# Attention of the later tiles: float32 products on quarters of the TensorE array instead of split float32r products

## The chip, the cores and the metric

The kernel runs on one core of one Trainium2 chip. The metric is device time in microseconds, from the start to the end of one execution. The kernel before takes 1346.17 us (median of 3 runs, 1345.73 to 1346.28).

## The reference, cut to what matters

Eight batches of 576 tokens with 8 heads of 64 features: attention within chunks of 64 tokens, then two feed-forward blocks on 4608 tokens of 512 features.

```python
q_c = q.reshape(B, H, nc, 64, 64)                 # the same for k, v
scores = scale * np.matmul(q_c, k_c.transpose(0, 1, 2, 4, 3))
scores = scores - np.max(scores, axis=-1, keepdims=True)
attn = np.exp(scores)
attn = attn / (np.sum(attn, axis=-1, keepdims=True) + 1e-09)
x = np.matmul(attn, v_c)                          # heads side by side: 4608 x 512
xn = (x - mu) / np.sqrt(var + 1e-06) * g_ln
x2 = x + np.maximum(xn @ w_ch1, 0.0) @ w_ch2      # 512 -> 2048 -> 512
h = np.maximum(x2 @ w_in, 0.0)                    # 512 -> 1024
out = h * sigmoid(conv3(h)) @ w_out               # taps over tokens; 1024 -> 512
```

All data is float32.

## The kernel before, in words

**Tiles and slabs.** Tokens go through in 36 tiles of 128 (two chunks of 64 each) and in nine slabs of four tiles. Phase A does attention and the first feed-forward block, phase B the second one. This case lies in phase A.

**The dense work.** A float32 operand is split into hi + lo, twelve leading bits each, so that TensorE can use single-pass float32r; one product is three matmuls (`mm3`, lines 100 to 103). For one slab, 16 groups f of 128 hidden features go by: `U(f)` (line 591, 12 matmuls of 512 columns into the PSUM tile `ups`), `H(f)` (line 605, ScalarE: relu, hi), `K(f)` (line 610, VectorE: lo), and `D(f)` (line 614, 12 matmuls into the four `acc` tiles). In the program `D(f-1)` comes after `U(f)`. The PSUM tile of `ups` has two buffers; attention has one buffer of two banks, tag `at` (`at_bank2`), which scores, transposes, values and two of the four feature transposes `xtp` share in turn.

**Attention of the next slab lies between the dense matmuls.** The order is written out by hand. Slab 0 follows the list START: it computes the attention of tiles 0 to 7 by class `Whole` (lines 278 to 413), in plain float32. `Whole.S` (line 317) multiplies 128 rows of block-diagonal q by 64 columns of k for each of 8 heads. `Whole.V` (line 372) multiplies operands of 64 rows, alternately in the upper and the lower half of the array's rows. `Whole.P` (line 353) transposes in float32. A plain float32 matmul shows in the trace as two records, each with its own weight load.

In slabs 1 to 7 `slot(t)` is called twice per f, after `K(f)` (t = 2f) and after `D(f-1)` (t = 2f + 1), so 12 dense matmuls lie between two slots. It runs class `Split` (lines 415 to 529) for the next slab's four tiles, in eight jobs of one tile and one parity of heads, three slots each:

- `load` fetches q, k and v of the job, each twice (to both halves of the partitions): 12 DMAs of 128 KB per tile, on SP's queue.
- `prep_qk`, `prep_v`: hi on ScalarE (lines 440, 441, 97), lo on VectorE (lines 442, 445, 98).
- `S` (line 472): four matmuls with 128 rows (q's hi above q's lo) and 256 columns; `fold` (lines 462, 464) adds the parts; maxima.
- `exp` (line 487): four ACTIVATEs with sums, then the division (lines 491 to 493). `parts` splits the weights (lines 97, 98).
- `P` (line 507): four float32r transposes, copied out at line 512.
- `V` (line 523): four matmuls of 256 columns, `fold` into x; for the second parity the statistics of layer normalization.

On VectorE, `late` holds four stores of the slab before (line 630, a transpose of 128 x 512, then a DMA); one is issued after each of K(0) to K(3), ahead of the slot.

Slab 8 has no attention beside it, and phase B starts behind it.

Of the kernel before, what the change touches and what calls it, by code (L numbers as in the profile page):

```python
# [17 lines left out]
# The first slab, step by step, in an order in which each engine finds its next step ready. Of a  # L18
# tile: L load, S scores, M maxima, E exponentials, N weights, P C transposed, V values, X B x and
# its statistics, x normalized, T transposed, p q hi and lo. Of a piece of the weights: W load,  # L20
# a t m to float32, h l hi and lo. Of 128 hidden features: U up, H K hi and lo, D down.
# [18 lines left out]
def attn_moe_moe2(  # L40
# [16 lines left out]
    """Tokens go through in tiles of 128, two chunks of 64 each, and in slabs of four tiles.  # L57

    q0, k0, the first tiles: tile, chunk c, d, parity e of the head, pair j (head 2j + e), row of
    the chunk; q, k, the others: tile, parity, d, pair, chunk, row; v: tile, parity, row, pair,  # L60
    chunk, d.
    A float32 is split exactly into hi + lo, twelve leading bits each, for the tensor engine's
    single-pass float32r: a product is lo*hi + hi*lo + hi*hi.
    """
# [21 lines left out]
    ident_r = const.tile([128, 128], F32R, name="ident_r")  # L86
# [18 lines left out]
    # -------------------------------------------------------------- weights  # L105
# [3 lines left out]
    class Piece:  # L109
        """w as float32, times scale, split into hi + lo, which take the place of w as it came."""  # L110
# [47 lines left out]
    def top_bits(y, raw):  # L158
        """Of a float64's top word: the float32 but for its last three bits, shifted right by 3."""
        # Of the exponents' difference, 1023 - 127, 112 * 8.  # L160
        nc.scalar.activation(
            out=y.bitcast(F32), in_=raw[..., 1].bitcast(F32), func=AF.Copy, scale=2.0 ** -112
        )

    def low_bits(raw):
        """Of a float64's low word: the float32's last three bits, rounded, with at most 7."""
        nc.vector.tensor_scalar(
            out=raw[..., 0], in0=raw[..., 0].bitcast(U32), scalar1=2.0 ** -29, scalar2=7.0,
            op0=ALU.mult, op1=ALU.min,
        )  # L170

    def to_f32(y, raw):
        """The shift drops the sign; the top word has it."""
        nc.vector.scalar_tensor_tensor(
            out=y, in0=y, scalar=3, in1=raw[..., 0], op0=ALU.logical_shift_left, op1=ALU.bitwise_or
        )
        nc.vector.scalar_tensor_tensor(
            out=y, in0=raw[..., 1], scalar=-0x80000000, in1=y, op0=ALU.bitwise_and, op1=ALU.bitwise_or
        )
# [27 lines left out]
    def cv_step():  # L207
        """A step of each of three pieces."""
# [22 lines left out]
    def add(w, parts, at, pool, tag, scale=None):  # L231
        """The [128, 512] block w for parts[at]: hi, lo."""
# [25 lines left out]
    # ------------------------------------------------------------ attention  # L258
# [19 lines left out]
    class Whole:  # L278
        """Attention of a whole tile in float32: few steps for the vector engine."""

        def __init__(self):
            self.pool = tc.alloc_tile_pool(name="at1", bufs=1, side="right", reuse_waits="tile")
            own = self.pool.tile([128, H, 128], F32, name="qbd")
            # The first tiles' q, block diagonal, where their features will be.
# [130 lines left out]
    class Split:  # L415
        """Attention by jobs of one tile and one parity of heads, for the fewest passes.

        The rows of a product's operands are the twelve-bit parts of q (of the weights) over d
        (over the keys); the columns hold k's (v's) parts beside each other.
        """  # L420

        def __init__(self):
            self.p = tc.alloc_tile_pool(name="at2", bufs=1, side="right", reuse_waits="tile")
            self.raw, self.qk, self.vv, self.st, self.x = {}, {}, {}, {}, {}

        def load(self, j):
            T, e = divmod(j, 2)
            for nm, src in (("q", q), ("k", k), ("v", v)):
                t = self.p.tile([128, 512], F32, tag="rw", bufs=6, name="rw" + nm)
                a = src[T if nm == "v" else T - N0, e].rearrange("p j c s -> p (j c s)")  # L430
                for x in range(2):
                    nc.sync.dma_start(out=t[half(x)], in_=a)
                self.raw[nm, j] = t

        def prep_qk(self, j):
            qr, kr = self.raw.pop(("q", j)), self.raw.pop(("k", j))
            qs = self.p.tile([128, HP, 128], F32R, tag="qs", name="qs")
            ks = self.p.tile([128, 2, HP, 128], F32R, tag="ks", name="ks")
            qf, kf = (t.rearrange("p j n -> p (j n)") for t in (qs, ks[:, 0]))
            nc.scalar.copy(qf, qr)  # L440
            nc.scalar.copy(kf, kr)
            nc.vector.tensor_tensor(
                out=qf[half(1)], in0=qr[half(1)], in1=qf[half(1)].bitcast(F32), op=ALU.subtract
            )
            nc.vector.tensor_tensor(
                out=ks[:, 1].rearrange("p j n -> p (j n)"), in0=kr, in1=kf.bitcast(F32), op=ALU.subtract
            )
            self.qk[j] = (qs, ks)

        def prep_v(self, j):  # L450
            vr = self.raw.pop(("v", j))
            vs = self.p.tile([128, 2, HP, 128], F32R, tag="vs", name="vs")
            f = [vs[:, i].rearrange("p j n -> p (j n)") for i in range(2)]
            split(f[0], f[1], vr)
            self.vv[j] = vs

        def fold(self, out, ps):
            """out[row, head] = the sum over the parts of the row's own chunk."""
            pv = ps.rearrange("p b (j i c n) -> p (b j) i c n", j=2, i=2, c=2)
            t = self.p.tile([128, HP, 64], F32, tag="c1", bufs=2, name="c1")  # L460
            for c in range(2):
                nc.scalar.copy(t[half(c)], pv[half(c), :, 1, c, :])
            for c in range(2):
                nc.vector.tensor_tensor(
                    out=out[half(c)], in0=pv[half(c), :, 0, c, :], in1=t[half(c)], op=ALU.add
                )

        def S(self, j):
            qs, ks = self.qk.pop(j)
            ps = at_bank2("sp")  # L470
            for h in range(HP):
                nc.tensor.matmul(  # L472
                    ps[:, h // 2, (h % 2) * 256:(h % 2) * 256 + 256], qs[:, h, :], ks[:, :, h, :],
                    start=True, stop=True,
                )
            s = self.p.tile([128, HP, 64], F32, tag="s", bufs=2, name="s")
            self.fold(s, ps)
            mx = self.p.tile([128, HP], F32, tag="mx", bufs=2, name="mx")
            sm = self.p.tile([128, HP], F32, tag="sm", bufs=2, name="sm")
            nc.vector.tensor_reduce(out=mx, in_=s, axis=AX.X, op=ALU.max)  # L480
            nc.vector.tensor_scalar_mul(out=mx, in0=mx, scalar1=-SCALE)  # L481
            self.st[j] = (s, mx, sm)

        def exp(self, j):
            s, mx, sm = self.st[j]
            for h in range(HP):
                nc.scalar.activation(  # L487
                    out=s[:, h, :], in_=s[:, h, :], func=AF.Exp, scale=SCALE, bias=mx[:, h:h + 1],
                    accum_out=sm[:, h:h + 1],
                )  # L490
# [3 lines left out]
                out=s, in0=s, in1=sm[:, :, None].to_broadcast([128, HP, 64]), op=ALU.mult  # L494
            )

        def parts(self, j):
            s = self.st.pop(j)[0]
            ph = self.p.tile([128, HP, 2, 64], F32R, tag="ph", bufs=2, name="ph")
            split(ph[:, :, 0, :], ph[:, :, 1, :], s)  # L500
            self.st[j] = ph

        def P(self, j):
            ph = self.st.pop(j)
            tp = at_bank2("tp")[:, 0, :]
            for h in range(HP):
                nc.tensor.transpose(  # L507
                    tp[:, h * 128:(h + 1) * 128].bitcast(F32R),
                    ph[:, h].rearrange("p i k -> p (i k)"), ident_r,
                )  # L510
            pt = self.p.tile([128, HP, 128], F32R, tag="pt", name="pt")
            nc.scalar.copy(pt.rearrange("p h t -> p (h t)"), tp)
            self.st[j] = pt

        def V(self, j):
            T, e = divmod(j, 2)
            pt, vs = self.st.pop(j), self.vv.pop(j)
            if e == 0:
                self.x[T] = x_tile()
            x = self.x[T]  # L520
            ps = at_bank2("pv")
            for h in range(HP):
                nc.tensor.matmul(  # L523
# [4 lines left out]
            if e:  # L528
                ln_stats(T, self.x.pop(T))
# [427 lines left out]
```

## Time and profile before

| | |
|---|---|
| median of 3 runs | 1346.17 us (1345.73 to 1346.28) |
| the profiled execution, first to last instruction | 1345.0 us, 18441 instructions |
| TensorE (matmul records) busy | 1325.9 us, 99% |
| VectorE, ScalarE, GpSimd busy | 871.7, 702.8, 81.1 us |
| mean granted TensorE clock | 0.985 of full |
| DMA queue of the data, share of 16 engines | 24.8% |

The profiled execution is one execution of its own; the page gives its time from the first to the last instruction, 1345.0 us, which is 1.2 us under the median of the runs. Matmuls are pipelined and the ends of their records are modelled, so records overlap, and a busy share of 99% doesn't say that the array computes all the time. What an operation costs TensorE is read from the starts of records: from its own first start to the start of what follows.

### The profile page before, as it was taken

The numbers are of one execution on the slowest core, as the hardware profiler recorded it, in microseconds if no ns is written. First come the engines' busy times: TensorE is split into PE (matmuls) and PEld (weight loads), VectorE is DVE, ScalarE is ACT, GpSimd is POOL, SyncE is SP. The second block draws the span as 40 slices with busy tenths as digits, with TensorE's granted clock in tenths as the row PEclk, the third lists the DMA queues.
The fourth block names the chain that finished last, engine by engine and source line by source line (L and its number), as shares of the span: only waits on it lengthen the run. The fifth ranks groups of instructions, "written<-read, shape, count | busy, mean of one in ns | idle before, by whom it ended". The sixth has DMA issues, their size and how long they took to land.

```text
span 1345.0 us, 18441 instructions
## 1 busy us (share of the span) xinstructions
PE 1325.9 (99%) x6312; PEld 1100.1 (82%) x6312; DVE 871.7 (65%) x1824; ACT 702.8 (52%) x1767; POOL 81.1 (6%) x176
## 2 busy tenths in 40 slices
PE   7899999999999999999999999999999999999998
PEld 6788788888888888888888888888788888888887
DVE  6898577566666666676676676555787556655550
ACT  5675366365365365365365365233576555555541
POOL 1000000000000000000000000000022111111100
PEclk6799999999999999999999999999999999999999
DMA  9812042132132132132132133141311111101001
GB/s 290 334 53 59 16 126 79 43 99 79 44 98 79 46 96 79 47 95 79 48 94 79 47 95 80 40 164 63 94 39 41 48 55 63 49 30 56 24 24 47
DMA packets 77661, 105.04 MB, mean 78 GB/s; under 512 B 20224, under 2 KB 38656, under 8 KB 77568
## 3 DMA queue, kind: packets, MB, share of 16 engines
q1 hardware_dynamic: 77568, 103.87, 24.8%
q8 instruction: 50, 0.82, 0.3%
q14 instruction: 43, 0.35, 0.1%
HBM read 84.96 MB, written 18.87 MB: 77 GB/s over the span
## 4 chain that ended last, share of the span: by engine, by line
PE 93%; DVE 4%; ACT 1%; DMA 1%; issue 1%; SPq 1%; DVEq 0%; ACTq 0%
PE ups L101 14%; PE ups L103 14%; PE ups L102 14%; PE acc L101 10%; PE acc L103 10%; PE acc L102 10%; PE ops L102 5%; PE ops L103 5%; PE ops L101 5%; PE sp L472 2%; PE pv L523 2%; PE xtp L563 1%; PE tp L507 1%; PE sp L317 1%; DMA w<-in_moe_w_ch_dram 0%
## 5 line engine op out<-in xcount | busy, mean ns | idle before, releaser
L101 PE MATMUL ups<-xh,w 128*128 128x512 f32 x656 | 260.6, 397 | 1.4 <-ACT xh L406 1.4
L103 PE MATMUL ups<-xh,w 128*128 128x512 f32 x656 | 258.2, 394 | 0.0
L102 PE MATMUL ups<-xl,w 128*128 128x512 f32 x656 | 257.1, 392 | 0.3 <-DVE xl L410 0.3
L101 PE MATMUL acc<-w,hl 128*128 128x512 f32 x576 | 229.5, 399 | 0.0
L103 PE MATMUL acc<-w,hh 128*128 128x512 f32 x576 | 225.3, 391 | 0.0
L102 PE MATMUL acc<-w,hh 128*128 128x512 f32 x576 | 225.1, 391 | 0.0
L605 ACT ACTIVATE hh<-ups 128x512 fp32r<-128x512 f32 x144 | 86.3, 599 | 237.6 <-PE ups L103 230.8
L610 DVE SCALAR_TENSOR_TENSOR hl<-ups,hh 128x512 fp32r<-128x512 f32 x144 | 99.6, 691 | 153.1 <-ACT hh L605 151.5
L103 PEld LDWEIGHTS ups<-xh,w 128*128 128x128 f32 x656 | 123.6, 188 | 27.8
L101 PEld LDWEIGHTS ups<-xh,w 128*128 128x128 f32 x656 | 123.9, 189 | 25.4 <-ACT xh L406 2.0
L102 PEld LDWEIGHTS ups<-xl,w 128*128 128x128 f32 x656 | 123.8, 189 | 25.3 <-DVE xl L410 1.1
L103 PEld LDWEIGHTS acc<-w,hh 128*128 128x128 f32 x576 | 108.2, 188 | 23.9
L101 PEld LDWEIGHTS acc<-w,hl 128*128 128x128 f32 x576 | 108.2, 188 | 19.9
L102 PEld LDWEIGHTS acc<-w,hh 128*128 128x128 f32 x576 | 108.4, 188 | 19.3
L840 DVE SCALAR_TENSOR_TENSOR cv<-hb,cw_sb,cv 128x510 f32<-128x510 f32 (+31 forms) x256 | 117.2, 513 | 0.6
L102 PE MATMUL ops<-w,Gh 128*128 128x512 f32 x288 | 112.0, 389 | 0.0
L101 PE MATMUL ops<-w,Gl 128*128 128x512 f32 x288 | 112.0, 389 | 0.0
L103 PE MATMUL ops<-w,Gh 128*128 128x512 f32 x288 | 112.0, 389 | 0.0
L487 ACT ACTIVATE s<-s,mx 128x64 f32<-128x64 f32 x224 | 74.9, 337 | 54.9 <-DVE mx L481 54.9
L855 DVE SCALAR_TENSOR_TENSOR gt<-cv,hb 128x512 f32<-128x512 f32 (+2 forms) x72 | 49.6, 689 | 50.6 <-ACT cv L850 50.6
L870 ACT CAST Gh<-gt 128x512 fp32r<-128x512 f32 (+5 forms) x96 | 46.9, 512 | 61.5 <-DVE gt L855 61.5
L275 POOL TENSOR_TENSOR rs<-rs,mhalf 128x1 f32<-128x1 f32 x36 | 23.5, 652 | 819.4 <-DVE rs L274 819.4
(115 smaller groups left out, 2145.9 us busy)
## 6 DMA issues: line engine op xcount, KB each, us to landing
w<-in_moe_w_ch_dram SPq DMA_DIRECT2D x32, 512.0 KB, 8.8
rwq<-in_q_dram SPq DMA_DIRECT2D x112, 128.0 KB, 2.7
rwk<-in_k_dram SPq DMA_DIRECT2D x112, 128.0 KB, 2.7
rwv<-in_v_dram SPq DMA_DIRECT2D x112, 128.0 KB, 2.7
x2d<-x2T SPq DMA_DIRECT2D x36, 256.0 KB, 2.0
x2r<-x2d SPq DMA_DIRECT2D x36, 256.0 KB, 3.9
out_dram<-ob SPq DMA_DIRECT2D x36, 256.0 KB, 2.0
w<-in_moe_w_out_dram SPq DMA_DIRECT2D x8, 512.0 KB, 5.2
```

The source lines that it names most:

```text
L101: nc.tensor.matmul(ps, ll, rh, start=first, stop=False)
L102: nc.tensor.matmul(ps, lh, rl, start=False, stop=False)
L103: nc.tensor.matmul(ps, lh, rh, start=False, stop=last)
L275: nc.gpsimd.tensor_tensor(out=rs, in0=rs, in1=mhalf, op=ALU.pow)
L472: nc.tensor.matmul(ps[:, h // 2, (h % 2) * 256:(h % 2) * 256 + 256], qs[:, h, :], ks[:, :, h, :], start=True, stop=True,)
L487: nc.scalar.activation(out=s[:, h, :], in_=s[:, h, :], func=AF.Exp, scale=SCALE, bias=mx[:, h:h + 1], accum_out=sm[:, h:h + 1],)
L523: nc.tensor.matmul(ps[:, h // 2, (h % 2) * 256:(h % 2) * 256 + 256], pt[:, h, :], vs[:, :, h, :], start=True, stop=True,)
L605: nc.scalar.activation(out=hh, in_=ps, func=AF.Relu)
L610: nc.vector.scalar_tensor_tensor(out=hl, in0=ps, scalar=0.0, in1=hh.bitcast(F32), op0=ALU.max, op1=ALU.subtract)
L840: nc.vector.scalar_tensor_tensor(out=cv[:, a:e], in0=hb[:, a + tap:e + tap], scalar=cw_sb[:, tap, f:f + 1], in1=cv[:, a:e], op0=ALU.mult, ...
L855: nc.vector.scalar_tensor_tensor(out=self.gt[:, j0:j1], in0=self.cv[:, j0:j1], scalar=1.0, in1=self.hb[:, j0 + 1:j1 + 1], op0=ALU.add, op1 ...
L870: nc.scalar.copy(Gh[self.f][:, r], g)
```

## The change

Class `Quad` takes the place of `Split` for tiles 8 to 35. It works on whole tiles, in plain float32, without splitting anything.

- `load`: one DMA of 256 KB each for q, k and v of a tile: parity e of the heads lies in partitions 64e to 64e + 63, each once.
- `quarters` issues, for each of four pairs j, four matmuls of 64 rows, 64 stationary and 64 moving columns: parity e picks the half of the array's rows and the PSUM bank, chunk c the half of its columns and of the PSUM partitions. So a product of a tile is 16 matmuls, and nothing is computed that isn't used.
- `session(tv, ts)` issues the values of tile tv and then the scores of tile ts into one `at` tile (the scores in the first half of each bank, the values in the second), the maxima of ts on VectorE, and one ScalarE copy of the values.
- One slot later `exp(ts)` (eight ACTIVATEs that read PSUM), the statistics of tv, and the load of tile tv + 2; two slots later `norm(ts)` on VectorE; three slots later `P(ts)`: four float32 transposes and a ScalarE copy.
- The sessions lie in slots 2, 10, 18, 26 of a slab (2, 8, 14, 20, 26 in slab 1, of which the first has scores alone). The last one of slab 7 has values alone: 29 sessions.
- `ident_r`, the identity as float32r, and the ScalarE cast that wrote it go away. START, the dense work, slab 8 and phase B stay as they are; comments are blanked.

```diff
-    ident_r = const.tile([128, 128], F32R, name="ident_r")
...
-    class Split:
...
+    class Quad:
...
+        def load(self, T):
+            for nm, src, to in (("q", q[T - N0], self.q), ("k", k[T - N0], self.k), ("v", v[T], self.v)):
+                t = self.p.tile([128, HP, 2, 64], F32, tag="r" + nm, bufs=2, name="r" + nm)
+                nc.sync.dma_start(
+                    out=t.rearrange("p j c s -> p (j c s)"),
+                    in_=src.rearrange("e p j c s -> (e p) (j c s)"),
+                )
+                to[T] = t
+
+        def quarters(self, ps, lt, rt):
+            for j in range(HP):
+                for e, c in ((0, 0), (1, 1), (0, 1), (1, 0)):
+                    nc.tensor.matmul(
+                        ps[half(c), e, j, :], lt[half(e), j, c, :], rt[half(e), j, c, :],
+                        start=True, stop=True,
+                    )
+
+        def session(self, tv, ts):
+
+            both = at_bank2("sv").rearrange("p e (i j n) -> p e i j n", i=2, n=64)
+            if tv is not None:
+                self.quarters(both[:, :, 1], self.st.pop(tv), self.v.pop(tv))
+            if ts is not None:
+                self.quarters(both[:, :, 0], self.q.pop(ts), self.k.pop(ts))
+                mx = self.p.tile([128, 2, HP], F32, tag="mx", bufs=2, name="mx")
+                nc.vector.tensor_reduce(out=mx, in_=both[:, :, 0], axis=AX.X, op=ALU.max)
+                nc.vector.tensor_scalar_mul(out=mx, in0=mx, scalar1=-SCALE)
+                self.st[ts] = (both[:, :, 0], mx)
+            if tv is not None:
+                x = x_tile()
+                nc.scalar.copy(x.rearrange("p (j e) d -> p e j d", e=2), both[:, :, 1])
+                self.st[tv] = x
...
+        def norm(self, T):
+            pp, sm = self.st.pop(T)
             nc.vector.tensor_scalar_add(out=sm, in0=sm, scalar1=1e-9)
             nc.vector.reciprocal(out=sm, in_=sm)
             nc.vector.tensor_tensor(
-                out=s, in0=s, in1=sm[:, :, None].to_broadcast([128, HP, 64]), op=ALU.mult
+                out=pp, in0=pp, in1=sm[:, :, :, None].to_broadcast([128, HP, 2, 64]), op=ALU.mult
             )
...
+            if si == 1:
+                plan = {2: (None, n0), 8: (n0, n0 + 1), 14: (n0 + 1, n0 + 2), 20: (n0 + 2, n0 + 3),
+                        26: (n0 + 3, n0 + 4)}
+            else:
+                plan = {2: (n0, n0 + 1), 10: (n0 + 1, n0 + 2), 18: (n0 + 2, n0 + 3), 26: (n0 + 3, n0 + 4)}
...
+                for at, (tv, ts) in plan.items():
+                    if ts == NTILE:
+                        ts = None
+                    if t == at:
+                        at2.session(tv, ts)
+                    elif t == at + 1:
+                        if ts is not None:
+                            at2.exp(ts)
+                        if tv is not None:
+                            at2.stats(tv)
+                            if tv + 2 < NTILE:
+                                at2.load(tv + 2)
+                    elif t == at + 2 and ts is not None:
+                        at2.norm(ts)
+                    elif t == at + 3 and ts is not None:
+                        at2.P(ts)
```

## Rows read from the trace of the kernel before

**Rows 1.** The page: busy time of each engine; granted clock in 40 slices.

```profile
PE 1325.9 (99%) x6312; PEld 1100.1 (82%) x6312; DVE 871.7 (65%) x1824; ACT 702.8 (52%) x1767; POOL 81.1 (6%) x176
...
PEclk6799999999999999999999999999999999999999
```

**Rows 2.** Busy time of each engine in one slab, with granted clock and DMA share.

```profile
core 0: us, PE busy (x) PEld busy (x) DVE busy (x) ACT busy (x) POOL busy (x), PEclk, DMA share, GB/s
448.60:549.34 100.74, 100.66 (x499) 83.81 (x497) 66.87 (x148) 53.49 (x156) 2.33 (x4) 1.00 0.25 74
```

**Rows 3.** Waits of PE over the span, the longest row: us in total, times, longest us.

```profile
PE sp L317 <- DMA kr<-in_k_dram: 3.1, 2, 1.8
```

**Rows 4.** Timeline of PE, slab 2: start, us, what, count. Values, then scores.

```profile
301.14 0.63 PE L523 MATMUL pv<-vs,pt 128*128 128x256 f32 x4
301.61 0.39 PE L101 MATMUL ups<-xh,w 128*128 128x512 f32 x1
...
304.37 0.64 PE L472 MATMUL sp<-ks,qs 128*128 128x256 f32 x4
304.84 0.40 PE L101 MATMUL acc<-w,hl 128*128 128x512 f32 x1
```

**Rows 5.** Timeline of PE, slab 2: the transposes of one job.

```profile
307.59 0.45 PE L507 MATMUL tp<-ident_r,ph 128*128 128x128 f32 x4
...
308.18 0.39 PE L102 MATMUL ups<-xl,w 128*128 128x512 f32 x1
```

**Rows 6.** Timeline of PE, slab 0: plain float32 scores on all 128 rows.

```profile
115.44 1.90 PE L317 MATMUL sp<-kr,qbd 128*128 128x64 f32 x16
...
117.46 0.39 PE L102 MATMUL ups<-xl,w 128*128 128x512 f32 x1
```

**Rows 7.** Timeline of PE, slab 0: plain float32 values, on row halves.

```profile
122.48 0.39 PE L103 MATMUL acc<-w,hh 128*128 128x512 f32 x1
122.80 1.16 PE L372 MATMUL pv<-vt,pt 64*128 64x128 f32 x16
...
124.23 0.40 PE L102 MATMUL ups<-xl,w 128*128 128x512 f32 x1
```

**Rows 8.** Those values' weight loads begun by three times: window, busy (count).

```profile
122.79:122.81 0.02, 0.01 (x2) 1.00 0.00 0
122.79:123.01 0.22, 0.21 (x4) 1.00 0.00 0
...
122.79:123.23 0.44, 0.43 (x8) 1.00 0.00 0
```

**Rows 9.** Timeline of PE, slab 0: plain float32 transposes.

```profile
112.22 0.60 PE L353 MATMUL tp<-ident,pp 128*128 128x128 f32 x4
...
112.90 0.40 PE L102 MATMUL acc<-w,hh 128*128 128x512 f32 x1
```

**Rows 10.** Timeline, slab 2: last matmul of a U, its relu, its K.

```profile
297.78 0.39 PE L103 MATMUL ups<-xh,w 128*128 128x512 f32 x1
...
298.21 0.60 ACT L605 ACTIVATE hh<-ups 128x512 fp32r<-128x512 f32 x1 [2.01 <-PE ups L103]
...
298.84 0.69 DVE L610 SCALAR_TENSOR_TENSOR hl<-ups,hh 128x512 fp32r<-128x512 f32 x1 [1.09 <-ACT hh L605]
```

**Rows 11.** Timeline of DVE: maxima and division in slab 0; K and store in slab 2.

```profile
117.37 0.69 DVE L323 TENSOR_REDUCE mx<-sp 128x8 f32<-128x512 f32 x1 [0.39 <-PE sp L317]
...
120.87 0.17 DVE L342 TENSOR_SCALAR sm<-sm 128x8 f32<-128x8 f32 x1
...
121.31 0.69 DVE L344 TENSOR_TENSOR pp<-pp,sm 128x512 f32<-128x512 f32 x1
...
257.90 0.69 DVE L610 SCALAR_TENSOR_TENSOR hl<-ups,hh 128x512 fp32r<-128x512 f32 x1 [2.36 <-ACT hh L605]
258.51 0.70 DVE L630 STREAM_TRANSPOSE x2T<-x 128x512 f32<-128x512 f32 x1
259.13 0.82 DVE L464 TENSOR_TENSOR s<-sp,c 64x256 f32<-64x256 f32 x2
```

More of the change, by code (lines that the diff above doesn't have):

```diff
@@ L413, in q @@
             )
-    class Split:
+    class Quad:
         def __init__(self):
             self.p = tc.alloc_tile_pool(name="at2", bufs=1, side="right", reuse_waits="tile")
[L424 to L465, printed above, removed]
-                )
[L468 to L490, printed above, removed]
@@ new lines, in __init__ @@
+            self.q, self.k, self.v, self.st = {}, {}, {}, {}
+        def load(self, T):
[4 more added lines that the diff above has]
+                    in_=src.rearrange("e p j c s -> (e p) (j c s)"),
+                )
+                to[T] = t
@@ new lines, in exp @@
+        def exp(self, T):
+            sp, mx = self.st.pop(T)
+            sm = self.p.tile([128, HP, 2], F32, tag="sm", bufs=2, name="sm")
+            pp = self.p.tile([128, HP, 2, 64], F32, tag="pp", bufs=2, name="pp")
+            for j in range(HP):
+                for e in range(2):
+                    nc.scalar.activation(
+                        out=pp[:, j, e, :], in_=sp[:, e, j, :], func=AF.Exp, scale=SCALE,
+                        bias=mx[:, e, j:j + 1], accum_out=sm[:, j, e:e + 1],
+                    )
+            self.st[T] = (pp, sm)
@@ L491, in exp, with stats @@
+        def stats(self, T):
+            ln_stats(T, self.st.pop(T))
+        def norm(self, T):
+            pp, sm = self.st.pop(T)
             nc.vector.tensor_scalar_add(out=sm, in0=sm, scalar1=1e-9)
@@ L493, in exp, with P @@
             nc.vector.tensor_tensor(
-                out=s, in0=s, in1=sm[:, :, None].to_broadcast([128, HP, 64]), op=ALU.mult
+                out=pp, in0=pp, in1=sm[:, :, :, None].to_broadcast([128, HP, 2, 64]), op=ALU.mult
             )
[L497 to L504, printed above, removed]
+            self.st[T] = pp
+        def P(self, T):
+            pp = self.st.pop(T)
             tp = at_bank2("tp")[:, 0, :]
-            for h in range(HP):
+            for j in range(HP):
                 nc.tensor.transpose(
-                    tp[:, h * 128:(h + 1) * 128].bitcast(F32R),
-                    ph[:, h].rearrange("p i k -> p (i k)"), ident_r,
-                )
[L511 to L523, printed above, removed]
-                    ps[:, h // 2, (h % 2) * 256:(h % 2) * 256 + 256], pt[:, h, :], vs[:, :, h, :],
-                    start=True, stop=True,
-                )
-            self.fold(x.rearrange("p (j e) d -> p e j d", e=2)[:, e], ps)
-            if e:
-                ln_stats(T, self.x.pop(T))
+                    tp[:, j * 128:(j + 1) * 128], pp[:, j].rearrange("p e k -> p (e k)"), ident
+                )
+            pt = self.p.tile([128, HP, 2, 64], F32, tag="pt", bufs=2, name="pt")
+            nc.scalar.copy(pt.rearrange("p j c r -> p (j c r)"), tp)
+            self.st[T] = pt
     with tc.manual_schedule():
@@ L540, in attn_moe_moe2 @@
         nc.gpsimd.memset(mhalf, -0.5)
-        nc.scalar.copy(ident_r, ident)
         for f in range(NF1):
@@ L690, in attn_moe_moe2 @@
                 cvp.release()
-                at2 = Split()
-                at2.load(16)
-                at2.prep_qk(16)
-                at2.load(17)
+                at2 = Quad()
+                at2.load(N0)
+                at2.load(N0 + 1)
             if not nxt:
@@ L700, in attn_moe_moe2 @@
             hid = Hidden()
-            start = 2 if si == 1 else 1
+            n0 = T0 + 4
+            if si == 1:
[3 more added lines that the diff above has]
+                plan = {2: (n0, n0 + 1), 10: (n0 + 1, n0 + 2), 18: (n0 + 2, n0 + 3), 26: (n0 + 3, n0 + 4)}
             def slot(t):
@@ L706, in slot @@
                     return
-                j0 = 2 * (T0 + 4)
-                if t < start:
-                    return
-                a, r = divmod(t - start, 3)
-                j = j0 + a
-                last = 2 * NTILE
-                if r == 0 and a < 8:
-                    at2.S(j)
-                elif r == 1:
-                    if a < 8:
-                        at2.exp(j)
-                    if 0 < a < 9:
-                        at2.P(j - 1)
-                    if a < 8 and j + 1 < last:
-                        at2.prep_qk(j + 1)
-                elif r == 2:
-                    if 0 < a < 9:
-                        at2.V(j - 1)
-                    if a < 8:
-                        at2.parts(j)
-                        at2.prep_v(j)
-                        if j + 2 < last:
-                            at2.load(j + 2)
+                for at, (tv, ts) in plan.items():
[14 more added lines that the diff above has]
+                        at2.P(ts)
             for f in range(NF1):
```

## The prediction

> **What bounds the kernel now.** I read the profile's page first: TensorE's records cover 99% of the span, VectorE's 65%, ScalarE's 52%, and the granted clock is full in all slices but the first two [rows 1]. Then the windows: one slab with attention beside it lasts 100.74 us, TensorE's records cover 100.66 of them at clock 1.00, and the DMA engines move data a quarter of the time [rows 2]. Then the waits: over the whole span the longest row of TensorE's is 3.1 us, for the first loads of k [rows 3]; from slab 1 to slab 7 it waits for nobody. So in slabs 1 to 7 time is TensorE's own stream, and whatever the change takes from ScalarE, VectorE and the queues is worth nothing by itself: 12 DMAs of 128 KB per tile that become three of 256 KB, the splits, the folds. I cost these at nothing because TensorE's stream hides them today and less of them remains. The cast of the identity that goes away is one ScalarE operation ahead of START, where TensorE waits for loads: nothing too.
>
> Two things count then: how long TensorE needs for a tile's attention, before and after, and whether the new chain makes it wait.
>
> **TensorE before, per tile.** An ordinary matmul of 512 columns takes one step of 0.23 us: from 301.61 to 304.37 us lie the 12 of a U, 2.76 us [rows 4]. A job's scores take 304.84 - 304.37 = 0.47 us, its values 301.61 - 301.14 = 0.47 us [rows 4]. Its transposes take, up to the second matmul behind them less one step (the start of the first is blurred, its record is longer), 308.18 - 307.59 - 0.23 = 0.36 us [rows 5]. A tile has two jobs: 2 x 1.30 = **2.60 us**.
>
> **TensorE after, per tile.** No row shows a product on a quarter; it has to be built from plain float32 in slab 0.
>
> Scores on all rows: 16 records from 115.44 to 117.46 - 0.23 = 117.23 us, 0.112 us each [rows 6]. A record loads 128 columns of weights and moves 64 columns.
>
> Values on row halves: 16 records with 128 columns loaded and 128 moved. Weight loads begin in pairs, two by 122.81, four by 123.01, eight by 123.23 us [rows 8]: a pair each 0.11 us. So the two row halves work at the same time, and each needs the same 0.112 us per record as the scores. Scores move half as many columns in the same time, so what sets 0.112 us there is the load of 128 columns; and because values move 128 columns at that pace too, load and move of one half overlap each other. The whole group lasts from the ordinary end of the matmul ahead, 122.48 + 0.23 = 122.71, to 124.23 - 0.23 = 124.00 us: 1.29 us [rows 7]. Eight pairs are 0.90 us; the other 0.39 us is the change into row halves and back, which TensorE cannot fill.
>
> The Trainium skill speaks against the overlap: TensorE: Matmul & The Clock Gate, Part 3, says that a weight load runs beside matmuls in flight only where the row group differs. By that rule a quarter would alternate load and move and the sum would be that of the first rival below, 1351 us; rows 6 and 8 contradict it, and the sum goes by them.
>
> A quarter's record loads 64 columns and moves 64, half of both: 0.056 us, an estimate by proportion from rows 6 to 8. A session has 32 matmuls, so 64 records. Bounds: all four quarters at once gives 16 rounds, 0.90 us; one record at a time gives 64 x 0.056 = 3.58 us; and 3.58 us is also what 128 instructions take at the densest rate that a row shows, 32 (16 loads, 16 matmuls) in 0.90 us. I take four at once: the order of the four matmuls visits both row halves and both column halves in turn, and the nearest row, values on two halves, shows full overlap of what uses different parts of the array. With the change of mode, 0.39 us as in slab 0, a session costs 1.29 us. The transposes return to plain float32: 112.90 - 112.22 - 0.23 = 0.45 us [rows 9]. A tile costs 1.29 + 0.45 = **1.74 us**, 0.86 less than before; 28 tiles give 24.1 us. One session more than tiles (29) is one more change of mode, 0.4 us.
>
> **The new chain.** After a session come D(f-1), U(f+1), D(f), 36 matmuls, and then the transposes need the divided weights. So these are due 36 x 0.23 = 8.28 us after the first of the 36. What is late? Not the eight exponentials: in slab 0 maxima and exponentials together take 3.5 us, from 117.37 to 120.87 [rows 11]; the maxima start behind K(f) and a store at the latest, some 0.9 us in, so the exponentials end by 4.4 us, and relu H(f+1), queued behind them on ScalarE, is due only at 5.7. On VectorE the division stands behind K(f+1). The last matmul of U(f+1) starts 23 x 0.23 = 5.29 us in; relu starts 298.21 - 297.78 = 0.43 us later, K 0.63 us after that [rows 10], at 6.35; the next operation 0.61 us later (258.51 - 257.90), and the three of the division last 121.31 + 0.69 - 120.87 = 1.13 us [rows 11]. They end at 8.09 us; with a weight load of about 0.11 us the transposes start at 8.2, just in time. In slots 2 to 5, though, a store stands behind K(2) and ahead of the division: 259.13 - 258.51 = 0.62 us more [rows 11], so the transposes start at 8.82, 0.54 us late, once in each of seven slabs: 3.8 us. Queued behind the waiting transposes on TensorE is the next U, so it is paid in full. Bounds: nothing (if the chain is a little faster) to 0.54 us at each of 28 tiles, 15.1 us.
>
> The values' copy has 8 us until the transposes want its bank; the statistics have three slots at the least, 8 us, until `normed` reads them; the loads six slots, 16 us. All three cost nothing; without that cover the transposes or the next session would wait.
>
> **The sum.** -24.1 + 0.4 + 3.8 = -19.9 us. The profiled execution's 1345.0 us would become 1325.1; its span stands 1.2 us under the median of the runs, so I forecast 1346.2 - 19.9 = **1326 us**.
>
> **Rivals.**
>
> *Column halves take turns.* If two quarters of the same row half cannot load at the same time, a session has 32 rounds: 1.79 + 0.39 = 2.18 us, a tile 2.63. Then 28 x 0.03 + 0.4 + 3.8 = +5.0 us, **1351 us**, slower. It decides from 1.61 us of records in a session on: 2.60 - 0.45 - 0.39 leaves 1.76, and the 4.2 us of waits and the extra mode change take 0.15 per tile. For it: no row shows column halves at all. Against: the row halves overlap fully.
>
> *Records follow each other at a least spacing.* Break-even is 1.61 us / 64 records = 0.025 us; a limit about there, above the 0.014 us of my forecast and below the 0.056 us mean spacing in rows 7 and 8, leaves **1346 us**. For it: 128 instructions come where 48 did. Against: the first two loads of rows 8 begin within 0.02 us. The Trainium skill, same page, Back-to-back issue gap, gives 25 ns as the least start-to-start distance however few the columns; by that figure the sum would be just this, no change. The pairs of rows 8 lie closer, but their mean doesn't, so the trace leaves it open.
>
> *No overlap at all,* or an issue rate no better than rows 7: 3.58 + 0.39 + 0.45 = 4.42 us per tile, 28 x 1.82 + 4.2 = +55 us, **1401 us**. Against it stand rows 8; for it, only that a mode with column halves has no row.
>
> *The division is late for each tile:* 15.1 instead of 3.8 us of waits with four quarters at once, **1338 us**. For it: the margin worked out above is 0.1 us. Against: each link of the chain is a row, and they add up to just in time.
>
> **How the numbers follow.** Forecast 0.47, column halves in turn 0.26, least spacing 0.10, no overlap 0.10, late division 0.07. I count 0.2% (2.7 us) as what a measurement can tell from no change. Faster: 0.47 + 0.07 and 0.02 of the spacing case, 0.56. Same: 0.07 of the spacing case and 0.02 of the column case, 0.09. Slower: the rest, 0.35. The forecast's own range is 1316 (no wait, 3.8 us less; the change of mode at half its price, 28 x 0.2 = 5.6 us less) to 1338 (late division). The range of 8 in 10 reaches on to 1354, past the column rival with a little for a mode change that costs more in quarters; it leaves out the case without overlap and little else. As cases of both signs hold most of the chance, 1316 to 1338 is the likeliest one's own range.
>
> **What would show it.** Right: in a window of one session, 64 records within 0.9 to 1.0 us, weight loads beginning four to a round of about 0.06 us; slabs 2 to 7 at about 98 us in place of 100.74; waits of TensorE only at the transposes of slot 5, near 0.5 us, on the division; clock 1.00 throughout. Two to a round: the first rival. Evenly spaced loads, whatever the quarter: the second. A wait on the division at all four tiles of a slab: the last. The forecast falls if a session lasts over 2 us, or if TensorE waits for a load, for the values' copy or for the exponentials.

## The result, and the profile after

The kernel after takes **1325.74 us** (median of 4 runs, 1323.87 to 1325.96) against 1346.21 us before: a ratio of 0.9849, 95% interval 0.9835 to 0.9863. Forecast were 1326 us, within 1316 to 1354.

First the page of after: busy time by engine, and the granted clock in 40 slices.

```profile
PE 1299.9 (98%) x7544; PEld 1063.5 (80%) x7544; DVE 622.8 (47%) x1236; ACT 510.3 (39%) x1318; POOL 79.1 (6%) x176
...
PEclk7799999999999999999999999999999999999999
```

Against [rows 1] VectorE does 249 us less and ScalarE 192 us less, TensorE issues 1232 matmul records more, and the clock is the same. The span falls by 21.0 us. TensorE's busy time falls by 26.0 us, more than the span: the gaps between its records grow by 5.0 us, for the most part in the waits below (3.3 us) and in slab 0 (2.5 us), whose steps the change leaves as they are.

One slab, in the columns of [rows 2], from its first feature transposes to those of the next:

```profile
441.51:539.07 97.56, 97.09 (x673) 78.78 (x672) 31.38 (x64) 26.03 (x92) 2.19 (x4) 1.00 0.13 44
```

97.56 in place of 100.74 us. The longest rows of TensorE's waits:

```profile
PE sp L316 <- DMA kr<-in_k_dram: 3.6, 3, 1.7
PE tp L486 <- DVE pp L477: 3.3, 7, 0.5
```

The first is in slab 0, as in [rows 3]. The second is new: seven waits of the transposes on the division.

**A session.** Timeline of PE: start, us, what, count.

```profile
404.68 0.39 PE L102 MATMUL ups<-xh,w 128*128 128x512 f32 x1
405.00 0.69 PE L437 MATMUL sv<-rv,pt 64*64 64x64 f32 x32
405.51 0.65 PE L437 MATMUL sv<-rk,rq 64*64 64x64 f32 x32
406.09 0.50 PE L100 MATMUL acc<-w,hl 128*128 128x512 f32 x1
406.42 0.40 PE L101 MATMUL acc<-w,hh 128*128 128x512 f32 x1
```

Read as in the prediction, from the full matmul ahead to the second one behind, each less one step: 406.42 - 0.23 - (404.68 + 0.23) = 1.28 us, where 1.29 was forecast. All 27 full sessions agree within 0.01 us. The weight loads begun by four times (window, busy, count in brackets):

```profile
404.98:405.02 0.04, 0.03 (x4) 1.00 0.00 0
404.98:405.08 0.10, 0.09 (x8) 1.00 0.00 0
404.98:405.13 0.15, 0.14 (x12) 1.00 0.00 0
404.98:405.19 0.21, 0.20 (x16) 1.00 0.00 0
```

Where [rows 8] have two loads to a round of 0.11 us, here are four to a round, and the session's 16 rounds begin 0.058 us apart. The matmuls of a round begin within 0.01 us of the loads of the next one, so all quarters load and multiply at once. The records don't name their quarter; that the four of a round lie in four quarters is read from the order in which they are issued, and the orders tried below bear it out.

**A session with one product**, the first of all:

```profile
160.04 0.39 PE L102 MATMUL ups<-xh,w 128*128 128x512 f32 x1
160.35 0.69 PE L437 MATMUL sv<-rk,rq 64*64 64x64 f32 x32
160.98 0.50 PE L100 MATMUL acc<-w,hl 128*128 128x512 f32 x1
161.31 0.40 PE L101 MATMUL acc<-w,hh 128*128 128x512 f32 x1
```

161.31 - 160.04 - 0.46 = 0.81 us. So a product is 1.28 - 0.81 = 0.47 us, eight rounds, and the change of mode is 0.81 - 0.47 = 0.34 us, as the prediction calls what a session costs beside its records.

**The wait.** VectorE, then TensorE, in slots 4 and 5 of a slab:

```profile
364.42 0.69 DVE L571 SCALAR_TENSOR_TENSOR hl<-ups,hh 128x512 fp32r<-128x512 f32 x1 [3.19 <-ACT hh L566]
365.03 0.70 DVE L591 STREAM_TRANSPOSE x2T<-x 128x512 f32<-128x512 f32 x1
365.65 0.13 DVE L475 TENSOR_SCALAR sm<-sm 128x8 f32<-128x8 f32 x1
365.82 0.20 DVE L476 RECIPROCAL sm<-sm 128x8 f32<-128x8 f32 x1
366.06 0.69 DVE L477 TENSOR_TENSOR pp<-pp,sm 128x512 f32<-128x512 f32 x1
```

```profile
366.04 0.39 PE L102 MATMUL acc<-w,hh 128*128 128x512 f32 x1
366.90 0.63 PE L486 MATMUL tp<-ident,pp 128*128 128x128 f32 x4 [0.47 <-DVE pp L477]
...
367.59 0.39 PE L101 MATMUL ups<-xl,w 128*128 128x512 f32 x1
```

K, store, division, transposes: each starts as the one ahead lets it go, and the transposes cost 367.59 - 366.04 - 0.46 = 1.09 us. In the same slab's third session, with no store in the way, they cost 415.19 - 414.23 - 0.46 = 0.50 us:

```profile
414.23 0.39 PE L102 MATMUL acc<-w,hh 128*128 128x512 f32 x1
414.49 0.63 PE L486 MATMUL tp<-ident,pp 128*128 128x128 f32 x4
...
415.19 0.40 PE L101 MATMUL ups<-xl,w 128*128 128x512 f32 x1
```

So the store costs 0.59 us, once a slab. But the division holds up these transposes too, by less than the view of waits shows. The transposes' first weight load begins 0.12 us after the division's end at 413.65 + 0.69 = 414.34, and not with the matmul ahead, at 414.23:

```profile
413.65 0.69 DVE L477 TENSOR_TENSOR pp<-pp,sm 128x512 f32<-128x512 f32 x1
414.46 0.42 PEld L486 LDWEIGHTS tp<-ident,pp 128*128 128x128 f32 x4 [0.27 <-issue]
```

All 28 sets of transposes begin 0.12 us after their division. In slab 0 [rows 9] the load begins with the matmul ahead, and a set costs 0.45 us; the second experiment takes this up.

### The profile page after: what moved, and what is told of

Same layout as the page of the kernel before. It is cut to its first block, busy times and chain, and to the rows that moved or that the text cites. A ratio compares the mean times of both kernels' runs of the same rounds, so it can differ in the third digit from the quotient of the medians.

```text
span 1324.0 us, 18972 instructions
## 1 busy us (share of the span) xinstructions
PE 1299.9 (98%) x7544; PEld 1063.5 (80%) x7544; DVE 622.8 (47%) x1236; ACT 510.3 (39%) x1318; POOL 79.1 (6%) x176
## 4 chain that ended last, share of the span: by engine, by line
PE 91%; DVE 5%; ACT 2%; DMA 1%; issue 1%; SPq 1%; ACTq 0%; DVEq 0%
PE ups L100 14%; PE ups L102 14%; PE ups L101 14%; PE acc L100 10%; PE acc L102 9%; PE acc L101 9%; PE ops L102 5%; PE ops L100 5%; PE ops L101 5%; PE sv L437 2%; PE xtp L524 1%; PE tp L486 1%; PE sp L316 1%; DMA w<-in_moe_w_ch_dram 1%; DVE cy L173 0%
## 5 line engine op out<-in xcount | busy, mean ns | idle before, releaser
L464 ACT ACTIVATE pp<-sv,mx 128x64 f32<-128x64 f32 x224 | 66.9, 334 | 2.2 <-DVE mx L451 2.2
```

The source lines that it names most:

```text
L464: nc.scalar.activation(out=pp[:, j, e, :], in_=sp[:, e, j, :], func=AF.Exp, scale=SCALE, bias=mx[:, e, j:j + 1], accum_out=sm[:, j, e:e + 1],)
```

## The experiments

All are edits of the kernel after. Single runs of one kernel lie up to 5.4 us apart. Much of it arises in slab 0, whose steps no edit touches: in the traces of these runs slab 1's feature transposes start anywhere from 142.29 to 146.23 us (145.91 in after). So each run is read in a slab's window too, from feature transposes to feature transposes (after: 97.56 us), and where the median says something else, from the start of slab 1 to the end of the trace (after: 1178.1 us).

### The store behind the slot's work

```diff
-                if late:
-                    late.pop(0)()
                 slot(2 * f)
+                if late:
+                    late.pop(0)()
```

Expected:

> The store of the slab before is issued behind the slot's attention work instead of ahead of it, so that in the first session of each of seven slabs it stands behind the division on VectorE. My theory: the 0.5 us waits of TensorE at the transposes (7 of them, 3.3 us in all, with 0.09 us each of load start on top) go, time falls by 3.5 to 4.1 us, to about 1322. Rival, that the wait comes from elsewhere (the exponentials, the maxima behind K): waits of 0.5 us stay and the time stays at 1326.

Measured: **1320.34 us** (1319.08 to 1321.40, 5 runs), ratio to the kernel before 0.9805, interval 0.9792 to 0.9818. The slab, then the transposes of the session in slot 2:

```profile
439.56:536.50 96.94, 96.94 (x673) 78.85 (x672) 31.31 (x64) 26.03 (x92) 2.19 (x4) 1.00 0.13 44
```

```profile
364.71 0.39 PE L102 MATMUL acc<-w,hh 128*128 128x512 f32 x1
364.98 0.63 PE L486 MATMUL tp<-ident,pp 128*128 128x128 f32 x4
...
365.68 0.40 PE L101 MATMUL ups<-xl,w 128*128 128x512 f32 x1
```

365.68 - 364.71 - 0.46 = 0.51 us: these transposes cost what the others cost, and TensorE's records cover the window without a gap, 96.94 of 96.94 us. A slab is 0.62 us shorter; seven make 4.3 us, and from slab 1 to the end the trace is 4.3 us shorter. The medians show 5.4, whose surplus is within the spread of the runs. The store was the cause of the 0.59 us.

### And the transposes one slot later

```diff
-                    elif t == at + 3 and ts is not None:
+                    elif t == at + (3 if at == 26 else 4) and ts is not None:
                         at2.P(ts)
```

Expected:

> As the run before, and the transposes one slot later (12 matmuls more after the division), but for the session in slot 26. If the transposes are only just in time where they do not visibly wait (they cost 0.51 us there, 0.45 by slab 0), 15 of them lose 0.06 us each: 0.9 us below the run before, about 1321. Rival, that 0.51 us is simply what four transposes cost between these neighbours: same as the run before.

Measured: 1321.10 us (1320.55 to 1321.99), ratio 0.9814, interval 0.9800 to 0.9827. The slab, then a set of transposes that was moved:

```profile
439.46:536.38 96.92, 96.92 (x673) 79.08 (x672) 31.31 (x64) 25.70 (x92) 2.19 (x4) 1.00 0.13 44
```

```profile
367.36 0.40 PE L102 MATMUL ups<-xh,w 128*128 128x512 f32 x1
367.37 0.59 PEld L486 LDWEIGHTS tp<-ident,pp 128*128 128x128 f32 x4
...
368.27 0.40 PE L101 MATMUL acc<-w,hh 128*128 128x512 f32 x1
```

The time is that of the run before, as the rival said, but its reason is refuted. With the division long done, the load begins with the matmul ahead and the set costs 368.27 - 367.36 - 0.46 = 0.45 us. So do all 22 sets that moved, while the six left in place cost 0.50 to 0.51. The neighbours are not the reason: in slab 1 of the run with extra work below, transposes in the old place, whose division ends at 186.43 + 0.69 = 187.12, only 0.05 us after the matmul ahead of them starts (0.11 us in the session shown above), cost 187.97 - 187.07 - 0.46 = 0.44 us:

```profile
186.43 0.69 DVE L485 TENSOR_TENSOR pp<-pp,sm 128x512 f32<-128x512 f32 x1
187.07 0.39 PE L102 MATMUL acc<-w,hh 128*128 128x512 f32 x1
...
187.97 0.39 PE L101 MATMUL ups<-xl,w 128*128 128x512 f32 x1
```

So the 0.05 us is a wait for the division, at every tile. A slab gains nothing by the move because what its three moved sets save, 0.17 us, comes back in the dense work, whose steps in this window take 0.16 us more in sum. Why they do stays open.

### Values and scores in two sessions

```diff
+        def values(self, tv):
+            both = at_bank2("sv").rearrange("p e (i j n) -> p e i j n", i=2, n=64)
+            self.both = both
             if tv is not None:
+                self.quarters(both[:, :, 1], self.st.pop(tv), self.v.pop(tv))
...
-                    if t == at:
+                    if t == at - 1:
+                        at2.values(tv)
+                    elif t == at:
                         at2.session(tv, ts)
```

Expected:

> Values one slot ahead of the scores instead of in one session with them: 27 changes of mode more. My theory: a change into quarters and back costs what the trace of after says, 2 x 0.822 - 1.289 = 0.355 us, so 27 x 0.355 = +9.6 us, about 1335; by slab 0 (0.39 us) +10.5 us. Rival, that the change is nearly free and the 0.35 us is the start of the first records: under +3 us, about 1328.

Measured: 1332.62 us (1329.99 to 1335.39), ratio 0.9899, interval 0.9881 to 0.9916: +6.9 us. The slab:

```profile
445.99:544.93 98.94, 98.46 (x673) 78.89 (x672) 31.00 (x64) 26.43 (x92) 2.19 (x4) 1.00 0.13 43
```

(98.94 - 97.56) / 4 = 0.345 us for each change of mode, as read from the one-product session; 27 of them are 9.3 us, and from slab 1 to the end the trace is 9.3 us longer. The median shows less, within the spread of the runs. So the price is real, and one session for two products earns 7 (by the median) to 9 us (by the traces) of the 20. The rival's +3 us is refuted, but not its reason: a start of the first records would be paid by each session as well. Against that reason speak the scores of slab 0, plain float32 on all rows without a change of mode: their weight loads begin 0.112 us apart, and 16 of them make 1.79 of the 1.80 us that the group costs, so next to nothing is left for a start. That it is the change of mode is argued from this; no run shows it alone.

### Work put back on ScalarE and VectorE

```diff
+        def extra(self):
+            a, b, c = self.junk
+            for _ in range(3):
+                nc.scalar.copy(b, a)
+                nc.vector.tensor_tensor(out=c, in0=a, in1=a, op=ALU.subtract)
...
+                    elif at < 26 and t in (at + 4, at + 5):
+                        at2.extra()
```

Expected:

> In the two slots behind the transposes of 22 sessions six casts of 128x512 on ScalarE and six subtractions of 128x512 on VectorE on a scratch tile are added, 132 of each: some 79 us of ScalarE and 91 us of VectorE, nearly half of what the change took from them. My theory: their load was hidden before and its removal brought nothing, so the time stays within 0.2% of 1326. Rival, that part of the gain is less work on these engines (memory ports, relu and lo on time): more than 3 us slower, up to half of the 20 us.

Measured: 1324.70 us (1323.13 to 1325.28), ratio 0.9838, interval 0.9824 to 0.9852. The slab:

```profile
440.20:537.73 97.53, 97.06 (x674) 78.85 (x673) 43.45 (x82) 36.88 (x110) 2.19 (x4) 1.00 0.13 44
```

12.1 us more on VectorE and 10.9 more on ScalarE in a slab (43.45 against 31.38, 36.88 against 26.03), and the slab is as long as before. That is a third of what the change took from VectorE in a slab (66.87 against 31.38) and two fifths of what it took from ScalarE (53.49 against 26.03), put where nothing waits for it. So the busy time taken from these engines is no part of the gain, as far as this goes. What stands ahead of what on VectorE does count, as the store showed.

### Other orders of the quarters

By column halves:

```diff
-            for j in range(HP):
-                for e, c in ((0, 0), (1, 1), (0, 1), (1, 0)):
+            for c in range(2):
+                for j, e in ((j, e) for j in range(HP) for e in range(2)):
```

Expected:

> Order of the 16 matmuls of a product: first the eight of chunk 0 (one column half, row halves in turn), then the eight of chunk 1. My theory, quarters that take their records from a deep common queue: a product stays at 8 rounds of 0.0585 us or little more, 1326 to 1330. Rival, that only what is issued close together overlaps: two quarters at a time, 16 rounds a product, 56 x 8 x 0.0585 = +26 us, about 1352.

By row halves:

```diff
-            for j in range(HP):
-                for e, c in ((0, 0), (1, 1), (0, 1), (1, 0)):
+            for e in range(2):
+                for j, c in ((j, c) for j in range(HP) for c in range(2)):
```

Expected:

> First the eight matmuls of parity 0 (one row half, column halves in turn), then the eight of parity 1. My theory as in the run before: 1326 to 1330. Rival, near neighbours alone: two quarters at a time, about 1352; and if column halves depend on the row halves' overlap, up to four times the rounds, 56 x 24 x 0.0585 = +79 us, about 1404.

Measured: 1334.42 us by columns (1333.93 to 1335.67), ratio 0.9917, interval 0.9900 to 0.9933, and 1336.03 us by rows (1333.98 to 1338.10), ratio 0.9927, interval 0.9907 to 0.9947. Neither theory: the price lies between. The slab by columns, and the weight loads begun in one of its sessions:

```profile
443.81:542.84 99.03, 98.56 (x673) 80.39 (x672) 31.66 (x64) 26.08 (x92) 2.19 (x4) 1.00 0.13 43
```

```profile
406.53:406.58 0.05, 0.03 (x2) 1.00 0.00 0
...
406.53:406.81 0.28, 0.26 (x10) 1.00 0.00 0
406.53:406.87 0.34, 0.32 (x14) 1.00 0.00 0
```

Five rounds of two loads, then one of four: the other column half joins when 10 of the 16 records ahead of it have begun their loads. A session grows by (99.03 - 97.56) / 4 = 0.37 us; by rows it is (99.10 - 97.56) / 4 = 0.39 us. From slab 1 to the end the traces are 10.7 and 11.0 us longer. The kernel issues all values of a session ahead of its scores, and by columns the records show that TensorE leaves this order:

```profile
406.55 0.80 PE L437 MATMUL sv<-rv,pt 64*64 64x64 f32 x26
407.14 0.27 PE L437 MATMUL sv<-rk,rq 64*64 64x64 f32 x2
407.18 0.28 PE L437 MATMUL sv<-rv,pt 64*64 64x64 f32 x3
```

Two records of the scores start while six of the 32 of the values are still to come. So a free quarter does get records ahead of their turn, but only from a few places behind. (The next expectation counts four rounds of two; the loads show five.) Two more runs ask how far. Neighbours that share a row half:

```diff
-                for e, c in ((0, 0), (1, 1), (0, 1), (1, 0)):
+                for e, c in ((0, 0), (0, 1), (1, 0), (1, 1)):
```

Expected:

> The four matmuls of a pair in the order upper rows left, upper rows right, lower rows left, lower rows right, so that neighbours share a row half. In the two runs that put one half of the array first, a product's first four rounds held two records, and four from the fifth on, when 8 of the 16 records ahead of the other half had begun: TensorE seems to look some 8 records ahead. My theory: the fourth quarter is only 6 records behind the first, in reach, so rounds of four throughout, slabs of 97.6 us, about 1326. Rival, that neighbours must share neither half: slabs of 99 us or more, 1335 to 1352.

Column halves in blocks of two pairs:

```diff
-            for j in range(HP):
-                for e, c in ((0, 0), (1, 1), (0, 1), (1, 0)):
+            for i, c in ((0, 0), (0, 1), (1, 0), (1, 1)):
+                for j, e in ((j, e) for j in (2 * i, 2 * i + 1) for e in range(2)):
```

Expected:

> By column halves again, but in blocks of two pairs: four matmuls (8 records) of the left half, then four of the right half. The other half is 8 records behind. If the reach is 8 records or a little more: nearly all rounds hold four records, slabs of 97.6 to 98.0 us, 1326 to 1329. Rival, a reach well under 8 records: each block begins with rounds of two, up to 12 rounds a product instead of 8, 56 x 4 x 0.0585 = +13 us, 1339, slabs near 99.4 us.

Measured: 1325.18 us (1323.38 to 1326.34), ratio 0.9848, interval 0.9832 to 0.9865, and 1326.07 us (1324.47 to 1326.85), ratio 0.9855, interval 0.9836 to 0.9873. Their slabs, in that order:

```profile
343.88:441.45 97.57, 97.10 (x673) 78.77 (x672) 31.39 (x64) 26.03 (x92) 2.19 (x4) 1.00 0.13 44
```

```profile
343.44:441.10 97.66, 97.18 (x673) 78.97 (x672) 31.38 (x64) 26.09 (x92) 2.20 (x4) 1.00 0.14 44
```

The first is the kernel after to 0.01 us: the diagonal order that I had named as a reason is not needed. With the other half 8 records behind, a slab loses 0.10 us, and a session, read as above, costs 1.33 us, 0.05 more; with 16 behind a slab loses 1.47 us. The reach lies around 6 to 8 records.

### Scores twice

```diff
+                self.quarters(both[:, :, 0], self.q[ts], self.k[ts])
                 self.quarters(both[:, :, 0], self.q.pop(ts), self.k.pop(ts))
```

Expected:

> The scores of each tile are issued twice (28 products more). My theory: a product costs 8 rounds of 0.0585 us = 0.468 us inside a session, so 28 x 0.468 = +13.1 us, about 1339. Rival, that a session's price is mostly the change of mode and the records are near free: under +5 us; rival, that the queue starves when 192 instructions come at once: over +20 us.

Measured: 1338.38 us (1335.30 to 1339.82), ratio 0.9948, interval 0.9929 to 0.9968: +12.6 us, where 13.1 was expected; from slab 1 to the end the trace is 13.1 us longer. The slab:

```profile
443.98:543.41 99.43, 98.96 (x801) 80.68 (x800) 31.67 (x64) 26.03 (x92) 2.19 (x4) 1.00 0.14 43
```

(99.43 - 97.56) / 4 = 0.47 us for 32 records more: eight rounds again. Neither free records nor a starving queue.

## Why the prediction was right

**The session** was the term that decided, built by proportion from plain float32 in slab 0, and it came within 0.01 us: 1.28 against 1.29. That closeness is luck in part, for two small errors cancel in it: a round is 0.058, not 0.056 us, and the change of mode 0.34, not 0.39 us.

**Column halves in turn** would have shown two loads to a round; four are there. The rule of the Trainium skill that was weighed (TensorE: Matmul & The Clock Gate, Part 3, a load overlaps only where the row group differs) does not hold here: each quarter loads 64 columns and moves 64 in one round of 0.058 us, and matmuls begin together with the loads of the next round, so a load runs beside its own half's matmuls.

**A least spacing.** 16 loads begin in 0.21 us, the 64 of a session in 0.89 us, 0.014 us each on average, and doubled scores keep that pace over 96 records. The 25 ns of the Trainium skill (same page, section Back-to-back issue gap) are no floor across quarters.

**The division**: 0.54 us once a slab were forecast; the store costs 0.59, in seven places, and the first run of the list showed it. The other 21 sets wait 0.05 us each, where the prediction had a margin of 0.1 us: so its last rival, a late division at all tiles, is true in small. **The transposes** cost the forecast 0.45 us where the division is done in time, 0.50 where it is not quite.

**The step that was mis-sized** is the price before, 2.60 us per tile. It held two jobs without disturbance and "it waits for nobody" from slab 1 to slab 7. The second is wrong. In the kernel before, TensorE, and VectorE a little ahead of it:

```profile
476.56 0.39 PE L103 MATMUL acc<-w,hh 128*128 128x512 f32 x1
477.03 0.71 PE L472 MATMUL sp<-ks,qs 128*128 128x256 f32 x4
...
477.81 0.39 PE L102 MATMUL ups<-xl,w 128*128 128x512 f32 x1
```

```profile
475.44 0.70 DVE L630 STREAM_TRANSPOSE x2T<-x 128x512 f32<-128x512 f32 x1
476.06 0.82 DVE L464 TENSOR_TENSOR x<-pv,c 64x256 f32<-64x256 f32 x2
```

These scores cost 477.81 - 476.56 - 0.46 = 0.79 us, 0.32 more than the 0.47 of [rows 4]. They share the one `at` buffer with the values ahead, whose fold on VectorE stands behind a store and ends at 476.88; the order of events says that this is the cause, though no run moved that store in the old kernel. The view of waits has no row for it; the trace calls the gap "issue". It comes once in each slab from slab 2 to slab 7, and with it a tile cost 2.71 us, counted as above over all groups of one slab: 8 scores 4.14, 8 transposes 2.95, 8 values 3.76 us, together 10.85 us, over four tiles. After, a slab's sessions and transposes cost 4 x 1.285 + 3 x 0.506 + 1.10 = 7.76 us. The difference is 3.09 us, and the slab is 3.18 us shorter; forecast were 4 x 0.86 - 0.54 = 2.9. So the old kernel was somewhat dearer than I had it, the new one too, and the sum, -19.9 against -20.5 us, is closer than its terms. Part of that is luck: from slab 1 to the end the trace of after is 21.9 us shorter than that of before, 1178.1 against 1200.0, and slab 0, which no term concerns, gave 0.9 us of it back in the span.

## What to carry to other kernels

Small plain float32 products can run on four quarters of the array at once, each with its own loads and matmuls: 64 x 64 x 64 took 0.47 us for 16 products, and the price to reckon beside it is 0.34 us for each stretch in quarters, so put products together in one. Let the four quarters take turns within about 6 to 8 matmul records of program order; which of them are neighbours didn't matter in the two orders tried. And when a chain through another engine is just in time, look for what stands ahead of it in that engine's queue: moving a store behind the division brought another 4 to 5 us, and 1320.34 us is the fastest version here. A view of waits without a row is no proof that nothing waits: compare a weight load's start with the end of what it needs.

## What was not expected of the hardware

- TensorE takes records out of program order for a free quarter, but only some 6 to 8 ahead: with the other column half 16 records behind, it joined after 10 loads had begun, and a session cost 0.37 us more; 8 behind, 0.10 us in a whole slab. Matmuls of the scores then start ahead of values that the kernel issued before them.
- The change into quarters and back costs 0.34 us, a little less than into row halves (0.39 us in slab 0), although the array is cut in both directions.
